# One list of steps up to the third batch's attention, one quad's sums moved to GpSimd, two late Q/K loads moved to ScalarE's queue

## The chip, the cores and the metric

The kernel runs on one core of a Trainium2 chip. The metric is the device time of one execution in microseconds (us); less is better. A core has five engines with an instruction queue each: TensorE (PE; its weight loads are listed as PEld), VectorE (DVE), ScalarE (ACT), GpSimd (POOL) and SyncE (SP). Each works through its own queue in program order and waits for the others by semaphores. DMA transfers are issued from the queues of SP, ACT and POOL.

## The reference

Cosine attention over 8 batches, 12 heads, 448 positions and 64 dimensions, followed by a two-layer network with an exact GELU. The heads of a batch lie side by side as 768 features of 3584 tokens.

```python
q_n = q / (np.linalg.norm(q, axis=-1, keepdims=True) + 1e-06)
k_n = k / (np.linalg.norm(k, axis=-1, keepdims=True) + 1e-06)
scores = np.matmul(q_n, k_n.transpose(0, 1, 3, 2)) / tau          # tau = 0.1
attn = np.exp(scores - np.max(scores, axis=-1, keepdims=True))
attn = attn / (np.sum(attn, axis=-1, keepdims=True) + 1e-09)
attn_out = np.matmul(attn, v)
x = attn_out.transpose(0, 2, 1, 3).reshape(B * S, H * D)          # 3584 x 768
h = x @ w_in                                                      # 768 -> 2048
g = 0.5 * h * (1.0 + erf(h / sqrt(2)))
out = g @ w_out                                                   # 2048 -> 768
```

## The kernel before

The heads are worked on in quads: 4 heads are one quad g, a batch is three quads, so there are 24 (g0 to g23). Batches are counted from 0 here: g0 to g2 are batch 0, g3 to g5 batch 1, g6 to g8 batch 2. A quad's 448 positions are seven chunks of 64.

**A quad's way.** `load_qk` brings Q and K (two DMAs of 448 KB) into one of four buffers; `square` (on ACT or POOL) and `reduce` (DVE) give the squared norms; `logs`, `roots` (ACT, logarithm and exponential, one table) and `inverses` (DVE) give one over the norm; `scale` (POOL) writes the normalised Q and K in bf16. They are turned either by PE (`transposes`, then `copies` by DVE out of PSUM) or, for most quads, by one DMA transpose from SP's queue. Then, chunk by chunk, `scores` (4 PE matmuls in 64x64 tiles into a pair of PSUM banks) and `exps` (ACT, one instruction for 128x896). `visit(p)` does scores and exponentials of the next chunk in pair p of three. The row sums are made on PE by `sums` (matmuls with ones, 16 a quad from batch 1 on) and turned on DVE (`turned`, `inverted`), or on POOL by `folded` (six additions of 128x896) followed by the longer `turned_all` and `inverted_all` on DVE. `values` weights V (28 PE matmuls), `spread` and `normalise` (DVE) write the batch's x. The squares and loads are numbered by unit: unit 0 and 1 are the halves of g0, unit n is g(n-1) from there on. The argument of `load_qk` is a quad.

**The network.** For each batch, 96 matmuls of 128x128x448 (16 row blocks m, six pieces kd of the 768 features) give h in PSUM banks, ACT applies the GELU into g. The output matmuls (128x384, 16 to a bank) of one batch are cut into single matmuls that are handed out between the `scores` of the next batch, as filling work; DVE copies a finished bank and SP stores it. ACT changes its table between exponentials and GELU; each change is one table load.

**Weights.** `load_wi(i)` brings w_in: 0 and 1 are features kd 0, 1 and kd 2, 3; 2 and 3 are kd 4, 5 for the first and second half of the columns. `load_wo(i)` brings w_out: 0 and 1 the two halves of kf for the first 384 output columns, 2 and 3 the same for the others. Both, and `load_v`, are issued from POOL's queue, which converts to bf16.

**The order of work.** The tile framework is told to keep the written order: each engine gets its instructions in the order in which the Python code calls the helpers. Batch 0's attention is a list of calls written out by hand (`attention_first`). What follows is code: `first(b)` for a batch's GELU layer, `attention(b, fill)` with branches for b = 1, b = 2 and the rest, and `upto(f, n)`, which calls a step for all units up to n that have not had it. In batch 1 every quad's sums are made on PE:

```python
    def both(g, p):
        total(g)
        weighted(g, p)
```

At the start `spin` gives PE matmuls without use, and `late` is a one-element POOL copy that reads g0's last K.

Of the kernel before, what the change touches and what calls it, by code (L numbers as in the profile page):

```python
# [9 lines left out]
F32 = mybir.dt.float32  # L10
# [6 lines left out]
def kernel(  # L17
# [108 lines left out]
    def load_qk(g):  # L126
        b, n = divmod(g, NQ)
        t = qkp.tile([128, 2, 2, C, D], F32, tag="qk", name=f"qk{g}")
        qk_t[g] = t
        for s0, s1 in ((0, 1), (1, 2)) if g == 0 else ((0, 2),):  # L130
            for i, src in enumerate((q, k)):
                eng = nc.scalar if g == 0 and s0 == 0 and i == 1 else nc.sync
                eng.dma_start(
                    out=t[:, i, s0:s1].rearrange("p s c d -> p s (c d)"),
                    in_=src[b, 4 * n + 2 * s0:4 * n + 2 * s1].rearrange(
                        "(s h) (p c) d -> (h p) s (c d)", h=2, c=C))
# [127 lines left out]

    def gathered(g, p):
# [58 lines left out]
    def values(g, chunks=range(C), p=None):  # L324
        for c in chunks:
            if c == 0 and g < NQ:
# [70 lines left out]
    def second_pieces(sb, t, ni):  # L397
        state = {}

        def mm(kf):  # L400
# [8 lines left out]
            if kf == KF - 1:  # L409
                nc.vector.tensor_copy(ot[:, ni * NH:(ni + 1) * NH], ps[:, :NH])  # L410
# [7 lines left out]
        return [lambda kf=kf: mm(kf) for kf in range(KF)]  # L418
# [46 lines left out]
    early = {}  # L465

# [5 lines left out]
    def attention_first():  # L472
        x_t[0] = xp.tile([128, KD, S], BF16, tag="x", name="x0")
        DV, AC, GP = nc.vector, nc.scalar, nc.gpsimd
        Q, K = 0, 1
        square(0, ((AC, Q),))
        square(0, ((AC, K),))
        reduce(0, Q)
        reduce(0, K)
        square(1, ((AC, Q),))  # L480
        upto(load_v, 1)
        logs(0)
        reduce(1, Q)
        roots(0)
        upto(load_wi, 1)
        square(1, ((AC, K),))
        inverses(0)
        square(2, ((AC, Q),))
        reduce(1, K)
        scale(0, ((GP, 1),))  # L490
        logs(1)
        reduce(2, Q)
        roots(1)
        scale(0, ((GP, 0),))
        spin(2)
        transposes(0, 1)
        square(2, ((AC, K),))
        inverses(1)
        spin(1)
        transposes(0, 0)  # L500
        square(3, ((AC, Q),))
        copies(0, 1)
        scale(1, ((GP, 0),))
        copies(0, 0)
        square(3, ((AC, K),))
        scale(1, ((GP, 1),))
        upto(load_qk, 5)
        spin(1)
        transposes(1, 0)
        reduce(2, K)  # L510
        scores(0, ((0, 0), (0, 1)))
        upto(load_v, 2)
        transposes(1, 1)
        copies(1, 0)
        logs(2)
        scores(0, ((0, 2), (0, 3)))
        roots(2)
        upto(load_wi, 2)
        exps(0, ((0, 0), (0, 1)))
        inverses(2)  # L520
        copies(1, 1)
        exps(0, ((0, 2), (0, 3)))
        spin(2)
        scores(0, ((0, 4), (0, 5)))
        scale(2, ((GP, 0),))
        reduce(3, Q)
        exps(0, ((0, 4), (0, 5)))
        spin(1)
        scores(0, ((1, 0), (1, 1)))
        reduce(3, K)  # L530
        exps(0, ((1, 0), (1, 1)))
        spin(1)
        scores(0, ((1, 2), (1, 3)))
        scale(2, ((GP, 1),))
        upto(load_qk, 6)
        transposes(2, 0)
        exps(0, ((1, 2), (1, 3)))
        sums(0, (0,))
        copies(2, 0)
        scores(0, ((1, 4), (1, 5)))  # L540
        logs(3)
        scores(0, ((0, 6), (1, 6)))
        roots(3)
        transposes(2, 1)
        exps(0, ((1, 4), (1, 5)))
        inverses(3)
        sums(0, (1,))
        scale(3, ((GP, 0),))
        copies(2, 1)
        sums(0, (2,))  # L550
        exps(0, ((0, 6), (1, 6)))
        sums(0, range(3, 5))
        scores(1, ((0, 0), (1, 0)))
        scores(1, ((0, 1), (1, 1)))
        sums(0, (5,))
        exps(1, ((0, 0), (1, 0)))
        sums(0, (6,))
        upto(load_wi, 3)
        transposes(3, 0)
        turned(0)  # L560
        exps(1, ((0, 1), (1, 1)))
        scores(1, ((0, 2), (1, 2)))
        values(0, (0,))
        scale(3, ((GP, 1),))
        upto(load_wi, 4)
        copies(3, 0)
        values(0, (1,))
        exps(1, ((0, 2), (1, 2)))
        values(0, (2,))
        scores(1, ((0, 3), (1, 3)))  # L570
        inverted(0)
        values(0, range(3, 5))
        spread(0, 1)
        values(0, (5,))
        exps(1, ((0, 3), (1, 3)))
        scores(1, ((0, 4), (1, 4)))
        values(0, (6,))
        spread(0, 0)
        sums(1, (0,))
        square(4, ((GP, K),))  # L580
        exps(1, ((0, 4), (1, 4)))
        sums(1, (1,))
        scores(1, ((0, 5), (1, 5)))
        normalise(0, 0)
        transposes(3, 1)
        exps(1, ((0, 5), (1, 5)))
        scores(1, ((0, 6), (1, 6)))
        copies(3, 1)
        sums(1, (2,))
        square(4, ((GP, Q),))  # L590
        square(5)
        upto(load_wo, 2)
        exps(1, ((0, 6), (1, 6)))
        sums(1, range(3, 5))
        normalise(0, 1)
        scores(2, ((0, 0), (1, 0)))
        sums(1, (5,))
        exps(2, ((0, 0), (1, 0)))
        sums(1, (6,))
        scores(2, ((0, 1), (1, 1)))  # L600
        turned(1)
        values(1, range(2))
        exps(2, ((0, 1), (1, 1)))
        values(1, (2,))
        scores(2, ((0, 2), (1, 2)))
        inverted(1)
        values(1, range(3, 5))
        spread(1, 0)
        values(1, (5,))
        exps(2, ((0, 2), (1, 2)))  # L610
        values(1, (6,))
        scores(2, ((0, 3), (1, 3)))
        sums(2, (0,))
        reduce(4, K)
        normalise(1, 0)
        exps(2, ((0, 3), (1, 3)))
        sums(2, (1,))
        scores(2, ((0, 4), (1, 4)))
        spread(1, 1)
        values(2, (0,))  # L620
        sums(2, (2,))
        exps(2, ((0, 4), (1, 4)))
        scores(2, ((0, 5), (1, 5)))
        normalise(1, 1)
        values(2, range(1, 3))
        exps(2, ((0, 5), (1, 5)))
        values(2, (3,))
        scores(2, ((0, 6), (1, 6)))
        exps(2, ((0, 6), (1, 6)))
        reduce(4, Q)  # L630
        spin(1)
        early[4] = mm_tile("hp0_4")[:, :S]
        w_in(0, early[4], 4, range(2))
        sums(2, range(3, 7))
        values(2, (4,))
        logs(4)
        turned(2)
        values(2, (5,))
        roots(4)
        values(2, (6,))  # L640
        inverted(2)
        inverses(4)
        scale(4)
        spread(2, 1)
        spread(2, 0)
        normalise(2, 1)
        normalise(2, 0)
        done.update({square: 6, reduce: 5, root: 5, scale: 5, transposes: 5})

# [49 lines left out]

    def attention(b, fill):
        fill = list(fill)
        if b == 1:
            parts = iter((20, 13, 14, 17, 16, 16))
        elif b == 2:
            parts = iter((22, 12, 12, 13, 11, 13, 11, 11, 11, 6, 6))
        elif len(fill) == 128:
            parts = iter((14, 22, 22, 26, 28, 16))
        else:  # L710
            parts = iter((14, 17, 13, 18, 18, 16))
# [28 lines left out]
        if b == 1:  # L740
            upto(scale, u + 3)
            upto(load_v, b + 2)
            upto(transposes, u + 3)
            upto(load_qk, g0 + NQ + 2)
            upto(square, u + 4)
            visit(0, 1, 2)
            run()
            visit(0, 1, 2)
            run()
            upto(load_qk, g0 + NQ + 3)  # L750
            visit(0, 1)
            upto(square, u + 5)
            run()
            visit(0, 1, 2)
            both(g0, 0)
            upto(load_v, b + 3)
            upto(load_qk, g0 + NQ + 4)
            visit(1, 2)
            upto(reduce, u + 4)
            run()  # L760
            visit(1, 2, 0)
            both(g0 + 1, 1)
            visit(2, 0)
            logs(6)
            roots(6)
            run()
            both(g0 + 2, 2)
            inverses(6)
            done[root] = 7
        elif b == 2:  # L770
            upto(scale, u + 3)
            upto(load_qk, g0 + 6)
            upto(transposes, u + 3)
            upto(scale, u + 4)
            upto(load_qk, g0 + 7)
            upto(transposes, u + 4)
            visit(0, 1, 2)
            run()
            visit(0, 1, 2)
            norms(9)  # L780
# [230 lines left out]
```

## Time and profile before

| | |
|---|---|
| runs | 402.37, 400.3, 406.49 us; median 402.37 |
| profiled execution | span 398.6 us from the first to the last instruction; 3.8 us less than the median of the runs, which also hold what lies around the span |
| busy | PE 392.0, PEld 207.8, DVE 264.0, ACT 267.8, POOL 250.6 us |
| granted TensorE clock | 0.999 on average |
| PE by kind | output matmuls 148.1 us, GELU layer 147.0, scores 46.0 and 9.5, values 24.2 and 17.5, sums 5.7 and 4.2, spins 8.7, transposes 5.5, last outputs 5.4 |
| DMA | 54.52 MB; hardware queue of SP 41.79 MB, software queue of POOL 11.80 MB |

A group's line gives engine, operation, out<-in by the program's names, shapes and count, then busy time and the mean of one in ns, then the idle time of the engine before it and what ended it. In a timeline the first column is the start, the second the length of the merged row. Rows of PE overlap by the depth of its pipeline, so what a row costs is the distance to the start of the next.

### The profile page before, as it was taken

Reading aid. Unit: us, or ns where it says so; the run is one execution under the profiler, and the core shown is the slowest. Engines: PE = TensorE matmul, PEld = TensorE weight load, DVE = VectorE, ACT = ScalarE, POOL = GpSimd, SP = SyncE. Lnnn points to the kernel's source line nnn. Section 1 sums busy time; section 2 is a strip of 40 time slices with the busy share of each in tenths; the row PEclk is TensorE's granted clock in tenths of the full one; section 3 lists DMA queues with packets and bytes.
Section 4 is the critical chain, followed back from the end, with each engine's and each line's share of the span. In section 5 each row is a group of like instructions: output and inputs, shape, how many; then the busy total and the mean of one; then the engine's idle time right before and its main releaser. Section 6 shows DMA issues by size and latency. Waiting matters only on the chain.

```text
span 398.6 us, 8027 instructions
## 1 busy us (share of the span) xinstructions
PE 392.0 (98%) x3245; PEld 207.8 (52%) x3245; DVE 264.0 (66%) x530; ACT 267.8 (67%) x399; POOL 250.6 (63%) x162
## 2 busy tenths in 40 slices
PE   7999999999999999999999999999999999999996
PEld 3444555555545555555555555555555555555564
DVE  5787214955487999589963999769973797461021
ACT  6995787557988877888665977889656756504300
POOL 5898814269699694959587394969768391920000
PEclk9999999999999999999999999999999999999999
DMA  8999999747296890678145591566024720130033
GB/s 290 261 258 217 205 233 308 154 106 226 50 254 234 158 230 2 178 150 207 70 105 138 126 240 38 162 113 147 2 27 101 148 46 2 41 77 3 1 80 80
DMA packets 66485, 54.52 MB, mean 137 GB/s; under 512 B 38672, under 2 KB 62352, under 8 KB 66448
## 3 DMA queue, kind: packets, MB, share of 16 engines
q1 hardware_dynamic: 54464, 41.79, 39.0%
q0 software_dynamic: 11600, 11.80, 18.8%
q8 instruction: 25, 0.41, 0.4%
q10 hardware_dynamic: 384, 0.43, 0.3%
q14 instruction: 12, 0.10, 0.1%
HBM read 45.61 MB, written 11.01 MB: 142 GB/s over the span
## 4 chain that ended last, share of the span: by engine, by line
PE 95%; issue 1%; DVE 1%; POOL 1%; ACT 0%; POOLq 0%
PE hp L469 37%; PE op L406 36%; PE st L242 9%; PE o L320 4%; PE o L335 4%; PE op L425 1%; PE sm L305 1%; PE sh L667 1%; PE tp L221 1%; PE sm L314 1%; PE spin L463 0%; POOL wi L441 0%; DVE nq L168 0%; POOL qkb L204 0%; POOL v L145 0%
## 5 line engine op out<-in xcount | busy, mean ns | idle before, releaser
L252 ACT ACTIVATE pt<-st 128x896 bf16<-128x896 f32 x155 | 132.5, 916 | 29.0 <-PE st L242 28.4
L406 PE MATMUL op<-wo,g 128*128 128x384 bf16 x864 | 148.1, 326 | 0.0
L469 PE MATMUL hp<-x,wi 128*128 128x448 bf16 x768 | 147.0, 353 | 0.1
L204 POOL TENSOR_TENSOR qkb<-qk,rn 128x896 bf16<-128x896 f32 (+1 forms) x50 | 80.2, 1628 | 66.3 <-DVE rn L188 64.9
L406 PEld LDWEIGHTS <-g 128*128 128x128 bf16 x864 | 81.4, 98 | 62.6 <-issue 11.2
L469 PEld LDWEIGHTS <-wi 128*128 128x128 bf16 x768 | 74.4, 98 | 71.1 <-issue 2.8
L263 POOL TENSOR_TENSOR acc<-acc,pt 128x896 f32<-128x896 f32 x55 | 103.8, 1887 | 4.3
L929 ACT ACTIVATE g<-hp 128x448 bf16<-128x448 f32 x128 | 63.6, 552 | 63.6 <-PE hp L469 63.5
L410 DVE COPY ot<-op 128x384 f32<-128x384 f32 x54 | 29.9, 555 | 83.1 <-PE op L406 80.8
L168 DVE TENSOR_REDUCE nq<-sq 128x14 f32<-128x896 f32 (+1 forms) x50 | 50.6, 1038 | 10.2 <-POOL sq L160 6.7
L242 PE MATMUL st<-qkT 64*64 64x448 bf16 x620 | 46.0, 356 | 0.2 <-ACT pt L252 0.2
L160 POOL TENSOR_TENSOR sq<-qk 128x896 f32<-128x896 f32 x18 | 29.9, 1683 | 16.3 <-DMA qk<-in_q_dram 10.9
L369 DVE TENSOR_TENSOR x<-o,rs 128x448 bf16<-128x448 f32 x48 | 28.0, 609 | 9.9 <-PE sh L667 6.4
L270 DVE TENSOR_TENSOR acc<-acc,pt 128x896 f32<-128x896 f32 x30 | 33.0, 1099 | 1.0
L158 ACT ACTIVATE sq<-qk 128x896 f32<-128x896 f32 (+1 forms) x32 | 27.8, 902 | 2.2 <-DMA qk<-in_q_dram 1.8
L364 DVE STREAM_TRANSPOSE rs<-rc 128x448 f32<-128x448 f32 x48 | 28.7, 626 | 0.6
L242 PEld LDWEIGHTS <-qkT 64*64 64x64 bf16 x620 | 17.9, 105 | 20.5 <-issue 12.7
L263 POOL TENSOR_TENSOR acc<-pt 128x896 f32<-128x896 bf16 x11 | 20.7, 1879 | 8.9 <-DVE x L369 8.9
L320 PE MATMUL o<-pt,v 64*64 64x448 bf16 x364 | 24.2, 351 | 0.0
L673 ACT ACTIVATE pt<-sh 128x448 bf16<-128x448 f32 x26 | 14.1, 544 | 9.2 <-PE sh L667 8.5
L276 DVE STREAM_TRANSPOSE ta<-acc 128x448 f32<-128x448 f32 x32 | 18.5, 617 | 0.2
L335 PE MATMUL o<-pt,v 64*64 64x448 bf16 x308 | 17.5, 351 | 0.5 <-DVE x L369 0.5
(54 smaller groups left out, 212.4 us busy)
## 6 DMA issues: line engine op xcount, KB each, us to landing
qk<-in_q_dram SPq DMA_DIRECT2D x23, 448.0 KB, 4.6
qk<-in_k_dram SPq DMA_DIRECT2D x23, 448.0 KB, 5.4
out_dram<-ot SPq DMA_DIRECT2D x48, 192.0 KB, 3.2
v<-in_v_dram POOLq DMA_DIRECT2D x7, 672.0 KB, 7.7
wo<-in_moe_w_out_dram POOLq DMA_DIRECT2D x4, 768.0 KB, 11.6
wi<-in_moe_w_in_dram POOLq DMA_DIRECT2D x4, 512.0 KB, 14.4
out_dram<-ot SPq DMA_DIRECT2D x12, 96.0 KB, 2.1
wi<-in_moe_w_in_dram POOLq DMA_DIRECT2D x4, 256.0 KB, 14.6
```

What stands on the lines that cost most here:

```text
L160: eng.tensor_tensor(sq, t, t, ALU.mult)
L168: nc.vector.tensor_reduce(nq_t[n][:, j, i], sq_t[g, i][:, s0:s1], mybir.AxisListType.X, ALU.add)
L204: eng.tensor_tensor(qkb[:, i, :, s0:s1].rearrange("p c s d -> p s c d"), t[:, i, s0:s1], rn[:, i].to_broadcast([128, s1 - s0, C, D]), ALU. ...
L242: nc.tensor.matmul(st[cols, n, :S], lhsT=qkT[rows, 1, c, cols], rhs=qkT[rows, 0, :, cols], start=True, stop=True, tile_position=(64 * s, 6 ...
L252: nc.scalar.activation(pt, st[:, :, :S], AF.Exp, scale=inv_tau)
L263: nc.gpsimd.tensor_tensor(acc_t[g], all_t[g][:, 0] if c == 1 else acc_t[g], all_t[g][:, c], ALU.add)
L270: nc.vector.tensor_tensor(acc_t[g], acc_t[g], all_t[g][:, c], ALU.add)
L320: nc.tensor.matmul(bank_t[g, h][64 * s:64 * (s + 1), :S], lhsT=v_t[g][rows, s, c, :], rhs=pt_t[g, s, c][rows], start=(c == 0), stop=(c == ...
L335: nc.tensor.matmul(bank_t[g, h][cols, :S], lhsT=v_t[g][rows, s, c, :], rhs=pt_t[g, s, c][rows], start=(c == 0), stop=(c == C - 1), tile_po ...
L406: nc.tensor.matmul(ps[:, :NH], lhsT=g_t[sb][:, kf, t * 128:(t + 1) * 128], rhs=wo[:, kf, ni * NH:(ni + 1) * NH], start=(kf == 0), stop=(kf ...
L469: nc.tensor.matmul(t, lhsT=wi[:, kd, m * 128:(m + 1) * 128], rhs=x_t[b][:, kd, :], start=(kd == 0), stop=(kd == KD - 1))
L929: nc.scalar.activation(g_t[sb][:, m, hf * S:(hf + 1) * S], hps.pop(m), AF.Gelu)
```

## The change

`attention_first`, the special cases of `first` for b = 0 and 1 and the branches of `attention` for b = 1 and 2 go. In their place `opening` is one list of 550 calls, from the first load to the end of batch 2's attention; `first(2)` and the later batches are as before. Helpers for single banks, matmul groups and GELUs (`bank`, `banks`, `mm`, `gelu`, `run`) let the list name them one at a time. Within the list: the first batches' squares, loads of weights and V, transposes and table loads stand in another order; the sums of g4 are made by `folded`; Q and K of g4 and g5 are loaded from ScalarE's queue after `roots(4)`; two output banks are evicted by ScalarE (`run(1, AC)`); g4's `values` come after all of batch 1's scores. Cut to its core:

```diff
-    def load_qk(g):
+    def load_qk(g, queue=None):
...
-                eng = nc.scalar if g == 0 and s0 == 0 and i == 1 else nc.sync
+                eng = queue or (nc.scalar if g == 0 and s0 == 0 and i == 1 else nc.sync)
...
-                nc.vector.tensor_copy(ot[:, ni * NH:(ni + 1) * NH], ps[:, :NH])
+                (nc.scalar.copy if eng is nc.scalar else nc.vector.tensor_copy)(ot[:, ni * NH:(ni + 1) * NH], ps[:, :NH])
...
+    def mm(b, m, k0, k1):
+        w_in(b, hps_t[b, m], m, range(k0, k1))
+    def gelu(b, m):
+        sb, hf = divmod(b, 2)
+        nc.scalar.activation(g_t[sb][:, m, hf * S:(hf + 1) * S], hps_t.pop((b, m)), AF.Gelu)
...
+    def opening():
+        spin(1)
+        load_qk(0)
+        square(1, ((GP, Q),))
+        table(EXP_SET)
...
+        load_qk(1)
+        load_v(0)
+        load_v(1)
+        square(0, ((AC, K),))
...
+        inverses(0)
+        load_wi(1)
+        reduce(1, K)
+        square(2, ((AC, Q),))
...
+        scale(0, ((GP, 1),))
+        inverses(1)
+        scale(0, ((GP, 0),))
...
+        scale(2, ((GP, 0),))
...
+        load_wi(0)
...
+        square(4, ((GP, Q),))
...
+        scale(3, ((GP, 0),))
...
+        scale(3, ((GP, 1),))
+        load_wi(3)
...
+        square(4, ((GP, K),))
...
+        exps(2, ((0, 6), (1, 6)))
+        bank(0, 4)
+        values(2, (3,))
...
+        logs(4)
+        roots(4)
+        load_qk(4, AC)
+        sums(2, (1,))
...
+        sums(2, (6,))
+        values(2, (4,))
...
+        values(2, (6,))
+        more(0)
+        normalise(2, 0)
+        load_wi(2)
+        bank(0, 5)
+        square(5, ((GP, Q),))
...
+        mm(0, 1, 0, 4)
+        mm(0, 4, 0, 2)
+        load_qk(5, AC)
...
+        mm(0, 0, 0, 4)
+        mm(0, 0, 4, 6)
...
+        late_copy()
+        square(5, ((AC, K),))
+        reduce(5, K)
+        load_wo(1)
+        gelu(0, 2)
+        mm(0, 5, 0, 6)
+        square(6, ((AC, Q),))
...
+        mm(0, 7, 0, 6)
+        gelu(0, 4)
+        scale(4, ((GP, K),))
+        transposes(4, 1)
...
+        square(6, ((GP, K),))
...
+        table(EXP_SET)
+        scale(4, ((GP, Q),))
+        load_wo(0)
+        mm(0, 9, 0, 6)
+        reduce(6, K)
+        logs(5)
+        roots(5)
+        table(GELU_SET)
+        gelu(0, 10)
+        transposes(4, 0)
...
+        copies(4, 0)
+        bank(0, 11)
+        reduce(7, K)
...
+        inverses(5)
...
+        load_v(2)
+        visit(2)
+        run(1)
+        scale(5, ((GP, Q),))
+        scale(5, ((GP, K),))
+        run(3)
+        load_wo(3)
+        run(5)
+        transposes(5)
...
+        sums(3)
+        load_wo(2)
+        turned(3)
...
+        folded(4, (1,))
+        folded(4, (2,))
...
+        folded(4, (6,))
+        turned_all(4)
+        inverted_all(4)
...
+        run(1, AC)
+        run(1)
+        visit(2)
+        visit(0)
+        values(4, p=1)
+        scale(7, ((GP, Q),))
+        table(GELU_SET)
+        values(5, p=2)
+        sums(5)
...
+    opening()
+    assert not todo_t, len(todo_t)
+    first(2)
+    for b in range(3, B):
+        attention(b, output_pieces(b - 1))
+        first(b)
```

## The prediction

> **What bounds the kernel now.** I read the page first (span, busy shares, chain that ended last), then the busy time by stretches, then the timelines of TensorE, ScalarE and GpSimd over the first 80 us, then the DMA landings.
>
> ```profile
> span 398.6 us, 8027 instructions
> ...
> PE 392.0 (98%) x3245; PEld 207.8 (52%) x3245; DVE 264.0 (66%) x530; ACT 267.8 (67%) x399; POOL 250.6 (63%) x162
> ...
> PE 95%; issue 1%; DVE 1%; POOL 1%; ACT 0%; POOLq 0%
> ```
>
> TensorE (PE) is busy for 392.0 of 398.6 us and carries 95% of the chain. By stretches:
>
> ```profile
> 2.00:4.00 2.00, 2.00 (x6) 0.82 (x6) 0.04 (x1) 0.48 (x1) 0.00 (x0) 1.00 0.92 296
> ...
> 10.00:20.00 10.00, 9.72 (x97) 4.45 (x98) 7.69 (x13) 9.14 (x15) 8.88 (x10) 1.00 1.10 261
> 20.00:30.00 10.00, 9.54 (x148) 4.46 (x147) 8.49 (x16) 9.37 (x12) 10.00 (x8) 1.00 1.10 258
> 30.00:40.00 10.00, 9.94 (x69) 4.69 (x64) 7.16 (x12) 5.95 (x12) 8.25 (x7) 1.00 1.20 216
> 40.00:50.00 10.00, 10.00 (x64) 5.55 (x63) 2.86 (x5) 7.08 (x12) 9.00 (x8) 1.00 1.31 205
> 50.00:60.00 10.00, 10.00 (x82) 5.04 (x81) 1.12 (x2) 8.66 (x11) 1.57 (x2) 1.00 1.22 233
> ```
>
> The first busy column is PE, the last three numbers are granted clock, DMA share and GB/s. Two different stages show. From 40 us on PE has no gap at all, so its time there is the sum of its instructions. Before 32 us its busy time says little: matmuls are issued in small groups with waits between them, while ScalarE is at 9.1 to 9.4 and GpSimd (POOL) at 8.9 to 10 of 10. The DMA engines are full (a share above 1) up to 60 us. The PE and ScalarE timelines tell what the early stage hangs on:
>
> ```profile
> 30.55 0.54 PE L469 MATMUL hp<-x,wi 128*128 128x448 bf16 x2
> 31.02 0.95 PE L305 MATMUL sm<-pt,ones 128*64 128x448 bf16 x8
> 31.89 0.76 PE L335 MATMUL o<-pt,v 64*64 64x448 bf16 x12
> 32.59 8.88 PE L469 MATMUL hp<-x,wi 128*128 128x448 bf16 x46
> ...
> 65.47 0.85 PE L314 MATMUL sm<-pt,ones 128*32 128x448 bf16 x16
> 66.25 1.52 PE L335 MATMUL o<-pt,v 64*64 64x448 bf16 x28
> ```
>
> ```profile
> 12.29 4.13 ACT L252 ACTIVATE pt<-st 128x896 bf16<-128x896 f32 x5
> ...
> 18.66 10.29 ACT L252 ACTIVATE pt<-st 128x896 bf16<-128x896 f32 x12 [0.16 <-PE st L242]
> 29.49 1.73 ACT L252 ACTIVATE pt<-st 128x896 bf16<-128x896 f32 x2 [0.55 <-PE st L242]
> ```
>
> ScalarE runs the first batch's 21 exponentials from 12.29 to 31.22, 0.857 us each in the long row (10.29 / 12). Right behind them PE sums and weights quad 2 and at 32.59 enters the first dense matmul block (46 in 8.88 us, 0.193 each). So the end is: start of that block, plus all PE work behind it, plus any hole that opens in it.
>
> **The change, part by part.**
>
> (1) PE work. The matmul sums of g4 (batch 1's second quad) go: 16 matmuls, from 65.47 to the next row at 66.25, **-0.8 us**. GpSimd takes six additions (g4 chunks 1 to 6) at 1887 ns, 11.3 us, in a stretch where it is busy 1.6 of 10. VectorE pays 4.0 us for turned_all and inverted_all (two transposes 0.61, one reduction 1.09, four of 0.17, four of 0.18, a reciprocal 0.33) for 2.0 before (0.65, 0.82, 0.21, 0.33): hidden, as it idles 80.8 us for output banks. Scores come in 10 groups in batch 1 for 8 now; a group of 12 takes 0.70 us to the next row, three times four matmuls at 0.19 are 0.57, so two more groups cost +0.2. The count of spins (29) and of all other matmuls is the same.
>
> (2) The opening. One half-quad square moves from ScalarE to GpSimd, and GpSimd issues load_v twice (0.89, 0.83) and load_wi (1.2 for its two) ahead of the first scale, for one load_v and one load_wi before. With the square from about 4.9 (0.9 by the half-size scale, 3.64 / 4) the first scale starts at 4.9 + 0.9 + 0.9 + 0.8 + 1.2 = 8.7 for 7.62 now, and the fourth ends at 12.3. The first scores need two of them: 10.5, plus a transpose 0.5, a copy 0.6, scores 0.5: exponentials from 12.15 for 12.29, because before they waited for a logarithm behind two squares. Then 21 x 0.857 = 18.0, logarithm and root 0.55, one wait for GpSimd's scale of quad 1 of 0.3: last exponential at 31.0. PE has then only one chunk of sums and three of values ahead (0.3 + 0.6; now three more chunks of sums): dense block at 31.9 for 32.59, **-0.7 us**. Bounds: if the exponentials slip by the whole 1.1 of the first scale, +0.4; -1.5 if their two waits (0.16 + 0.55) vanish also.
>
> (3) Weights and late Q, K. These are the edits that can open holes.
>
> ```profile
> L133 SPq DMA_DIRECT2D qk<-in_q_dram x25: 367/532/1453, 0.7 to 253.9; - x25
> ...
> DMA to landing us min/median/max: 3.3/5.0/17.0
> ...
> L448 POOL DMA_DIRECT2D wo<-in_moe_w_out_dram x4: 883/914/962, 30.0 to 41.1; - x4
> ...
> DMA to landing us min/median/max: 8.5/11.6/13.8
> ...
> L216 SPq DMA_TRANSPOSE qkT<-qkb x20: 1468/1496/8077, 46.3 to 318.9; - x20
> ...
> DMA to landing us min/median/max: 3.4/3.5/12.3
> ```
>
> These are the loads of Q and K, of w_out, and the DMA transposes, each with its time from issue to landing. The queues' own rows give rates: software queue alone 0.82 MB in 4 us (36 to 40 us), hardware queue alone 1.51 MB in 4 us; together they take turns (416 and 409 packets from 20 to 24).
>
> The last part of w_in that block 0 needs, load_wi(2), is now behind square(4) and scale(3) on GpSimd: 12.3 + 3.4 (two scales) + 1.2 (load_wi) + 1.7 (square) + 3.4 + 1.2 + 1.7 = 24.9 instead of 19.3. It is read when PE has done 20 matmuls of the block: 31.9 + 3.8 = 35.7. By the landing of the last two w_in loads (14.3 to 14.7) it comes at 39.5, a hole of 3.8; by the rates, 3.8 MB go through the software queue from 9 us on, 2.1 of them in 15 us shared with Q and K loads at 0.14 MB/us (0.45 and 0.67 MB in the 4 us from 20 and from 24), the rest at 0.2: 9 + 15 + 8.5 = 32.5, or 35 with 2 to 3 us lost between issues, none. I take none, since the 14 us were spent behind other weights and the loads of g4 and g5, which now leave at 31.5; only g6's leave SP early, at about 22, when scale(3) frees a buffer (counted in the 15 us).
>
> Those two leave from ScalarE's queue, after the last exponential and root: four issues of 0.41 (its one issue at 0.74 us), 1.6 us in an idle time of ScalarE (3.98 before the first gelu), so no cost there. But square(5) of Q on GpSimd waits for g4, and **behind it on GpSimd's queue stand** load_wo(1), scale(4,K), square(6,K), scale(4,Q), load_wo(0). With the median 5.0 the data lands at 36.5; 1.7 + 0.2 + 0.9 + 1.7 give scale(4,K) at 41.0. PE wants it for its transposes after 48 matmuls, at 31.9 + 9.2 = 41.1. At the 8.8 that g6's Q took at 50 us, beside load_v, it is 3.7 too late; only the tail of load_wi(2) is beside it here, so I take a landing of 6.0: **+0.9**. Then square 1.7 and scale 1.7 put load_wo(0) at 44.4. The first output matmul, run(1), stands behind 96 matmuls, two transposes (0.5 each) and three scores (0.7): 31.9 + 18.4 + 1.0 + 0.7 = 52.0. By its rows load_wo(0) lands 8.5 to 13.8 later, 52.9 to 58.2: a hole of 0.9 to 6.2. Those rows had 0.7 to 1.4 MB queued ahead (3.3 to 7 us at 0.2 MB/us); without that 5 to 7 are left, landing 49.5 to 51.5, none. I take **+0.5**.
>
> transposes(5), which makes g4's keys, moves from 46.3 to about 53 (its scale waits for inverses(5), on VectorE behind the copy of the last transposes and reduce(7,K), which ends at 48.9), and g4's first scores come after 30 output matmuls and 7 scores, at 58.1. The two DMA transposes of this stage landed in 8.3 and 12.3 us, later ones in 3.5: 56.5 to 65.3, a hole of 0 to 7.2. The 12.3 stood behind Q and K loads on the SP queue, which now are not ahead of it, and the first issued for 3.6 us; I take 5.5, **+0.4**. Holes overlap: PE that waited 2 us for one transfer finds the next landed. So they count as a maximum more than a sum, somewhat above the largest: **+1.5** for all, bounds 0 and 7.2.
>
> (4) The rest. Evicting two output banks on ScalarE (0.55 each) and the other squares there sit beside 26 us of PE work for some 20 of ScalarE. From batch 1's dense block on the list keeps the old order of matmuls, and the quads' normalised x is wanted after 11 output matmuls (1.9 us) plus five more among dense ones: VectorE's 3.3 behind sums(5) is covered.
>
> **Sum** against the profiled span: 398.6 - 0.8 + 0.2 - 0.7 + 1.5 = 398.8. The median of the runs, 402.4, is 3.8 above that span; kept, this gives 402.6 us.
>
> **Rivals.**
>
> *A visible hole, below 2%.* A landing comes at the middle of its rows (w_out 11.6, transpose 8.3, Q 8.8), 3 to 4 us late: 402.4 - 1.3 + 3 to 4, or 5 to 6 with a second one behind it: 404.5 to 407. For it: full DMA until 60 us. Against: less is queued ahead now.
>
> *The late Q and K hold up GpSimd.* One mechanism: g4 lands late from ScalarE's queue, square(5) blocks GpSimd, scale(4,K) and load_wo(0) slip, and PE stops before its transposes at 41 us. At the longest landing in the row, 17.0, data comes at 48.5, 12.0 late: 402.4 - 1.3 + 12.0 = 413.1 us. It passes 2% from a landing of 14.4 us. For it: that 17.0 occurred in this very stage, beside weights. Against: load_wi(2) should be the only competitor. In the trace PE's first spins ran 6 in 2 us, where 10.4 fit later, so a cold PE is nearly half as fast. The Trainium skill, "TensorE: Matmul & The Clock Gate", section "What's actually happening", says that one idle window of about 3.4 us puts the clock back to half until a busy window has passed; by that rule a hole of 12 us would cost up to 1.7 us more, 414.8. No run here shows it in mid-kernel.
>
> *The opening shrinks by far more.* Reaching 394 needs the dense block at 24 us. 21 exponentials of 0.857 cannot be done by then from 12 us on; only something unseen would do it: 393.
>
> *The additions do not save PE time* (the sums were in the shadow of something): 403.4, inside the forecast's case.
>
> **How the numbers follow.** Forecast (397 to 404.5) 0.52; hole below 2% 0.18; GpSimd held up 0.24; far shorter opening 0.06. The 2% (8 us) is about what a measurement of this kernel can tell from no change. So faster 0.06, same 0.70, slower 0.24. The range 396.5 to 411.5 leaves out the shorter opening and half of the third case.
>
> **What would show it.** Right: first dense matmul near 31.9, 64 of the 128x32 matmul sums in place of the 80 of L314, six more GpSimd additions, PE without idle rows over 1 us. Wrong: PE waiting for w_in at 36, for GpSimd's qkb at 41, for w_out at 52 or for qkT at 58 us; GpSimd's squares waiting on Q/K past 40 us; PE clock below 1 in mid-kernel.

## The result and the profile after

| | before | after |
|---|---|---|
| median of 6 runs each | 403.09 us | 414.62 us |
| profiled execution, span | 398.6 us | 411.7 us |
| ratio after / before | | 1.0334, interval 1.0302 to 1.0366 |

The changed kernel is slower by 3.3%. The ratio leaves out the runs of either kernel that lay more than 1.5% above its fastest (421.71 us after, for one), so it is not the ratio of the two medians. The page of the changed kernel's profile begins so (busy time and share by engine, then the granted clock in 40 slices, then the shares of the chain that ended last):

```profile
span 411.7 us, 8011 instructions
PE 394.4 (96%) x3229; PEld 207.9 (51%) x3229; DVE 265.3 (64%) x533; ACT 273.6 (66%) x407; POOL 251.1 (61%) x162
PEclk9999996999999999999999999999999999999999
PE 86%; DMA 5%; POOL 3%; ACT 3%; DVE 2%; issue 1%; DVEq 0%; POOLq 0%
```

PE's busy time rose by only 2.4 us while the span rose by 13.1, so most of the loss is idle PE. The chain that ended last, which held no DMA before, now holds 5% of it. And one slice of the clock, the seventh (62 to 72 us), is at six tenths. All three point at one place. PE's timeline there (start, length of the merged row, and in brackets the idle time before it with what ended it):

```profile
51.76 0.76 PE L242 MATMUL st<-qkT 64*64 64x448 bf16 x12
...
57.44 1.47 PE L411 MATMUL op<-wo,g 128*128 128x384 bf16 x8
64.66 0.96 PE L242 MATMUL st<-qkT 64*64 64x448 bf16 x8 [5.75 <-DMA qkT<-qkb]
65.55 1.50 PE L319 MATMUL sm<-pt,ones 128*32 128x448 bf16 x16
...
73.63 0.57 PE L242 MATMUL st<-qkT 64*64 64x448 bf16 x8
77.33 2.29 PE L411 MATMUL op<-wo,g 128*128 128x384 bf16 x13 [3.13 <-DMA wo<-in_moe_w_out_dram]
```

In the kernel before, PE worked through this place without a stop:

```profile
56.12 2.29 PE L406 MATMUL op<-wo,g 128*128 128x384 bf16 x13
58.33 0.76 PE L242 MATMUL st<-qkT 64*64 64x448 bf16 x12
59.03 2.45 PE L406 MATMUL op<-wo,g 128*128 128x384 bf16 x14
61.41 0.57 PE L242 MATMUL st<-qkT 64*64 64x448 bf16 x8
```

After, PE stops twice in batch 1's attention: 5.75 us for the turned keys of g4, then 3.13 us for the other half of w_out. Behind the first it runs at half speed: eight scores take 0.96 us at 64.66 and 0.57 at 73.63. The windows show it in their seventh figure, the granted clock (length, busy time and count of PE, PEld, DVE, ACT, POOL, then clock, DMA share, GB/s):

```profile
55.00:60.00 5.00, 3.91 (x32) 1.60 (x30) 1.55 (x2) 4.50 (x6) 3.09 (x3) 1.00 1.29 154
60.00:65.00 5.00, 0.34 (x4) 0.19 (x8) 0.00 (x0) 0.00 (x0) 0.00 (x0) 0.70 1.38 133
65.00:70.00 5.00, 5.00 (x43) 1.82 (x36) 2.72 (x9) 3.66 (x5) 2.80 (x2) 0.62 1.70 143
...
62.00:68.00 6.00, 3.34 (x33) 0.97 (x34) 0.85 (x3) 2.31 (x4) 0.88 (x1) 0.50 1.43 111
```

From 60 us until PE starts again at 64.66 no engine computes, while DMA is full. The last row, of a finer window, has the clock at 0.50. What the transfers do there is told by the landing rows (name, count, duration of the issuing instruction, then the time from issue to landing):

```profile
L453 POOL DMA_DIRECT2D wo<-in_moe_w_out_dram x4: 937/940/962, 37.5 to 57.2; - x4
DMA to landing us min/median/max: 7.6/10.5/20.1
...
L216 SPq DMA_TRANSPOSE qkT<-qkb x20: 1469/1498/6811, 53.0 to 331.2; - x20
DMA to landing us min/median/max: 3.4/4.4/16.3
```

The longest w_out load went from 13.8 to 20.1 us and the longest DMA transpose from 12.3 to 16.3, though the medians moved by about 1 us only (11.6 to 10.5, 3.5 to 4.4). Both extremes lie in this stage: the transpose of g4's keys, issued at 53.0 us, took 11.6, that of g5's, at 57.2, took 16.3; `load_wo(3)`, at 52.9, took 11.3 and `load_wo(2)`, at 57.2, took 20.1. The two transposes alone (duration of the issuing instruction in ns, then landing):

```profile
L216 SPq DMA_TRANSPOSE qkT<-qkb x2: 1606/3434/5261, 53.0 to 57.2; - x2
...
DMA to landing us min/median/max: 11.6/14.0/16.3
```

Each transpose leaves SP at the end of a pair of scales on GpSimd, and the next instruction on GpSimd's queue after that pair is a w_out load, so each pair starts together. The two queues then take turns, as the DMA view of 56 to 61 us shows (queue: packets, MB, share):

```profile
q0 software_dynamic: 818, 0.63, 87.2%
q1 hardware_dynamic: 829, 0.21, 43.9%
```

Nearly equal counts of packets, but the transposes' are some 256 bytes (0.21 MB / 829), and a transpose has some 1,800 of them (448 KB of bf16 for a quad's Q and K). The counts are not level everywhere: from 62 to 64 us they are 120 and 364, and why both queues moved less there stays open. In the kernel before, all four w_out loads had left GpSimd by 41.1 us and g4's transpose left SP at 46.3. In the view of the kernel before from 50 to 54 us the hardware queue, with that transpose, has most of the packets:

```profile
q1 hardware_dynamic: 1810, 0.46, 87.3%
q0 software_dynamic: 357, 0.26, 42.6%
```

**Where the 13.1 us went**, from the starts of PE's rows after, less those before: dense block of batch 0 -0.28; the way to batch 1's first scores +0.79; from there through batch 1's attention and dense block to batch 2's first scores +10.35; from batch 2's first scores to its dense block +1.42 (1.05 of it a wait for VectorE's write of x, up to 133.46 us); the end of the program +0.8. The 10.35 is 5.75 + 3.13 for the two waits, 2.07 for half speed (the work from 64.66 to 68.8 us in twice its time), less some 0.6, the remainder, which is about what the sums that left PE save.

These terms lie one behind the other on PE, but they are not independent causes. The 5% of DMA on the chain that ended last is one transfer, `load_wo(2)` (start and length):

```profile
57.15 20.13 DMA wo<-in_moe_w_out_dram
```

The chain runs through it and not through the wait for g4's keys. Without that wait and the half speed PE would have come to the other half of w_out at about 66.4 us (77.33 - 5.75 - 3.13 - 2.07), and a `load_wo(2)` that landed at the same 77.28 would by itself have held it for 10.9. This is an estimate from these rows; it supposes that the landing would not move.

### The profile page after: what moved, and what is told of

It reads as the page before. It is cut to its first block, busy times and chain, and to the rows that moved or that the text cites. A ratio compares the mean times of both kernels' runs of the same rounds, so it can differ in the third digit from the quotient of the medians.

```text
span 411.7 us, 8011 instructions
## 1 busy us (share of the span) xinstructions
PE 394.4 (96%) x3229; PEld 207.9 (51%) x3229; DVE 265.3 (64%) x533; ACT 273.6 (66%) x407; POOL 251.1 (61%) x162
## 4 chain that ended last, share of the span: by engine, by line
PE 86%; DMA 5%; POOL 3%; ACT 3%; DVE 2%; issue 1%; DVEq 0%; POOLq 0%
PE hp L472 33%; PE op L411 32%; PE st L242 7%; DMA wo<-in_moe_w_out_dram 5%; PE o L325 4%; PE o L340 3%; PE spin L468 2%; POOL qkb L204 2%; PE op L430 1%; PE sh L518 1%; ACT L480 1%; PE tp L221 1%; ACT pt L252 1%; ACT g L501 1%; PE sm L319 1%
## 5 line engine op out<-in xcount | busy, mean ns | idle before, releaser
L263 POOL TENSOR_TENSOR acc<-acc,pt 128x896 f32<-128x896 f32 x60 | 113.1, 1885 | 4.7
L415 DVE COPY ot<-op 128x384 f32<-128x384 f32 x52 | 28.9, 555 | 78.2 <-PE op L411 73.0
L242 PE MATMUL st<-qkT 64*64 64x448 bf16 x620 | 47.7, 362 | 7.2 <-DMA qkT<-qkb 5.8
L158 ACT ACTIVATE sq<-qk 128x896 f32<-128x896 f32 (+1 forms) x38 | 34.2, 921 | 4.3 <-DMA qk<-in_k_dram 1.8
L263 POOL TENSOR_TENSOR acc<-pt 128x896 f32<-128x896 bf16 x12 | 22.5, 1877 | 17.9 <-ACT pt L252 9.0
L160 POOL TENSOR_TENSOR sq<-qk 128x896 f32<-128x896 f32 (+1 forms) x12 | 19.3, 1623 | 19.7 <-DMA qk<-in_q_dram 15.5
L325 PE MATMUL o<-pt,v 64*64 64x448 bf16 x364 | 24.2, 351 | 0.0
L281 DVE STREAM_TRANSPOSE ta<-acc 128x448 f32<-128x448 f32 x34 | 19.6, 616 | 0.7 <-POOL acc L263 0.4
## 6 DMA issues: line engine op xcount, KB each, us to landing
wo<-in_moe_w_out_dram POOLq DMA_DIRECT2D x4, 768.0 KB, 10.5
```

The source lines that it names most:

```text
L158: eng.activation(sq, t, AF.Square)
L242: nc.tensor.matmul(st[cols, n, :S], lhsT=qkT[rows, 1, c, cols], rhs=qkT[rows, 0, :, cols], start=True, stop=True, tile_position=(64 * s, 6 ...
L263: nc.gpsimd.tensor_tensor(acc_t[g], all_t[g][:, 0] if c == 1 else acc_t[g], all_t[g][:, c], ALU.add)
L325: nc.tensor.matmul(bank_t[g, h][64 * s:64 * (s + 1), :S], lhsT=v_t[g][rows, s, c, :], rhs=pt_t[g, s, c][rows], start=(c == 0), stop=(c == ...
```

## The experiments

Two theories stood at the start. **A**: the transposes of g4 and g5 and the late w_out loads meet and delay one another. **B**: the late Q and K from ScalarE's queue delay GpSimd's scales, and all else follows. Diffs are against the changed kernel where nothing else is said. Medians of the kernel before, beside these runs, were 400.9 to 401.1 us.

**Q and K from SP, early (`e1_qk_from_sp`).** Part of the change undone.

```diff
         load_qk(3)
+        load_qk(4)
...
         scale(2, ((GP, 0),))
+        load_qk(5)
...
-        load_qk(4, AC)
...
-        load_qk(5, AC)
```

> The changed list, but Q and K of g4 and g5 leave from SP's queue early again (g4 behind g3, g5 behind the last scale of g1's successor). Theory A, the collision of the g4 and g5 DMA transposes with load_wo(3) and load_wo(2): GpSimd's squares no longer wait near 27 us, so load_wo(1) and load_wo(0) leave earlier, but scale(5) still waits for inverses(5) at about 49, so transposes and the two late load_wo still leave together near 53 and PE still stands 4 to 6 us at the first scores of g4 and about 3 us at the first output matmul of the second half: 412 to 415 us. Theory B, the late Q and K hold up all that follows on GpSimd: with them early the holes close, about 402 us.

Measured 414.74 us, ratio 1.0347 (1.0323 to 1.0371). Its PE timeline keeps both waits:

```profile
64.90 0.96 PE L242 MATMUL st<-qkT 64*64 64x448 bf16 x8 [5.73 <-DMA qkT<-qkb]
...
78.12 3.27 PE L411 MATMUL op<-wo,g 128*128 128x384 bf16 x13 [3.85 <-DMA wo<-in_moe_w_out_dram]
```

B falls for the change as it stands: with Q and K early, both waits stay.

**w_out early (`e2_wo_early`).** The other half.

```diff
         load_wi(2)
+        load_wo(0)
+        load_wo(1)
+        load_wo(2)
+        load_wo(3)
```

(and the four later calls removed)

> The changed list, but all four load_wo stand right behind load_wi(2), at about 27 us, where GpSimd idles 8.8 us; Q and K of g4 and g5 stay on ScalarE's queue at 32 us. Theory A: no w_out traffic is left at 53 us, the transposes land within 4 to 5 us, both holes go (5.75 and 3.1 us) and the half clock with them (2 us); but the late Q and K now share the DMA engines with w_out from 32 us, so that the transposes on PE at 41 us may wait 1 to 4 us: 402 to 406 us. Theory B: Q and K even later, so the hole at 58 us is as long or longer: 413 us or more.

Measured 410.32 us, 1.0238 (1.0217 to 1.0258). Both waits are gone, and the transposes, issued at 60.5 and 63.8 us, land in 3.5 and 3.4. These two leave 3.3 us apart, nearer than the 4.2 in the kernel after, so it is not each other's company that makes them slow there. But one new wait stands earlier on PE:

```profile
46.93 0.90 PE L221 MATMUL tp<-ident,qkb 128*128 128x128 bf16 x7 [4.66 <-ACT g L501]
```

PE waits there for banks that GELUs on ScalarE have to free. The chain of waits goes back from it: the GELUs stood behind ScalarE's square of g5's Q, and that Q, issued from ScalarE's queue at 33.62 us, took 11.42 to land, now that w_out shared the DMA engines with it. The clock is at 0.57 on average from 44 to 52 us. So A is right about the two waits, and early w_out alone trades them for a delay by late Q and K as in B, only that it stops ScalarE's queue where B had GpSimd's.

**Both early (`e3_both_early`).** The diffs of the first two together.

> Both edits together: Q and K of g4 and g5 from SP early, and all four load_wo behind load_wi(2). Theory A and B alike: both holes, the half clock and any wait at 41 us are gone, what is left of the change is one quad's sums less on PE: 401 to 403 us. If neither is right the holes stay and it is 410 us or more. The price that could show is load_wi(2) landing later than 36 us behind Q and K.

Measured 403.76 us, 1.0072 (1.0051 to 1.0094); the profiled span is 402.5, the clock 1.0 throughout. Of the 13.1 us, 9.2 are gone. Some of what is left, on PE:

```profile
37.52 5.46 PE L472 MATMUL hp<-x,wi 128*128 128x448 bf16 x28 [1.66 <-DMA wi<-in_moe_w_in_dram]
...
61.16 0.57 PE L242 MATMUL st<-qkT 64*64 64x448 bf16 x8 [0.84 <-DMA qkT<-qkb]
```

The first is the wait for `load_wi(2)` that the prediction had looked for at 36 us; it comes when other loads stand beside it.

**Matmuls without use in the first hole (`e4_spins_in_hole`).** `spin(28)` between `run(8)` and the `visit(1)` of g4's first scores, so that PE does not fall idle.

> The changed list with 28 further matmuls without use (5.4 us) put where PE stands still, ahead of g4's first scores. If the half clock after the hole (6.8 us of it in the profile, about 4 of them with work) costs time of its own, the clock stays at 1.0 and the time falls by about 2 us: 412.5 us. If the half clock costs nothing, since PE waits for w_out afterwards anyway, the time stays within 0.5 us of 414.6.

The time is unsettled: the four runs spread from 409.9 to 418.4 us, by more than the question. The profile, of the run of 416.64 us, still says something. The clock stayed at 1.00 from 62 to 76 us, so the half speed in the kernel after does come from the idle time. But PE stopped again for the same load:

```profile
77.77 4.34 PE L411 MATMUL op<-wo,g 128*128 128x384 bf16 x13 [3.31 <-DMA wo<-in_moe_w_out_dram]
```

It went on at 77.77, where the kernel after did at 77.33: in this execution what was saved ahead of `load_wo(2)` ran into the wait for it, and the half speed then followed that wait (0.57 on average from 76 to 84 us).

**Transposes on PE (`e5_pe_transposes`).** g4 and g5 turned by PE and copied by VectorE; the loads stay where they are.

```diff
-        transposes(5)
         run(7)
+        transposes(5, 1)
+        copies(5, 1)
+        transposes(5, 0)
+        copies(5, 0)
```

(the same for g5)

> The changed list, but g4 and g5 are turned by PE (28 small matmuls in four groups, about 0.45 us each, and four VectorE copies) where the two DMA transposes were; load_wo(3) and load_wo(2) leave at 53 and 57 us as in the changed kernel. Theory A (transposes and w_out slow each other down): with the transposes gone, load_wo(2) lands 7 to 8 us after its issue instead of 20, both holes go, and PE pays 1.8 us: 411.7 - 5.75 - 2.1 - 3.1 + 1.8, a span of 402.5, time 404.5 us. Rival, load_wo(2) is late because it is issued late behind GpSimd's scales: it lands near 77 us all the same and the time stays above 411 us.

Measured 411.41 us, 1.0227 (1.0148 to 1.0307). The half of A that only this run can show holds: without DMA transposes beside them `load_wo(2)` lands in 10.0 us in place of 20.1 and `load_wo(3)` in 9.5 for 11.3, though both leave as late as in the kernel after. The landing row of w_out:

```profile
DMA to landing us min/median/max: 9.5/10.5/11.1
```

The time is far above what was expected, because the removed waits left others:

```profile
55.03 4.16 PE L411 MATMUL op<-wo,g 128*128 128x384 bf16 x16 [1.95 <-DMA wo<-in_moe_w_out_dram]
...
68.86 0.55 PE L221 MATMUL tp<-ident,qkb 128*128 128x128 bf16 x7 [2.02 <-DVE ot L415]
```

`load_wo(0)` met g6's Q and K, which left SP at 44 us here, and PE's own transposes waited for a bank that VectorE had to empty. Behind each wait, of some 2 us, the clock was at half for 3.4 us. The transposes' own work on PE (some 2 us) comes on top.

**Only `load_wo(2)` and `load_wo(3)` earlier (`e11_wo_ahead_of_scale5`).** They move directly behind `load_wo(0)`, so that they no longer leave with the transposes but stand ahead of them.

```diff
         load_wo(0)
+        load_wo(2)
+        load_wo(3)
```

(and the two later calls removed)

> The changed list with only load_wo(2) and load_wo(3) moved, from behind scale(5) and scale(6) to directly behind load_wo(0) (45 us). They then go through the software queue from 50 to 58 us, so the g4 transpose at 53 us still meets w_out: it lands 10 us or more after its issue and PE's wait at 58 us stays (4 to 6 us, and the half clock behind it), but load_wo(2) lands by 62 us, so the wait for it at 74 us (3.1 us) goes: 411.5 us. If the order of issue alone mattered and not the meeting, both waits would go: about 403 us.

Measured 411.44 us, 1.0251 (1.0205 to 1.0297), as expected. The wait for w_out is gone, that for g4's keys is longer, since its transpose still takes 13.0 us beside the same loads:

```profile
65.48 0.96 PE L242 MATMUL st<-qkT 64*64 64x448 bf16 x8 [7.16 <-DMA qkT<-qkb]
```

So the first wait is a matter of what is still in the software queue when the transpose leaves, not of the order of the two issues.

**The collision in the kernel before (`e8_before_late_wo`).** There the late w_out loads move behind g4's DMA transpose.

```diff
-            upto(load_wo, 4)
...
                 if b == 0:
+                    upto(load_wo, 4)
```

> The kernel before, with one edit: load_wo(2) and load_wo(3) are issued behind the scale of g4, together with its DMA transpose (46 us), instead of 6 us earlier. Theory A: the two slow each other down here too: the transpose of g4 lands more than 10 us after its issue instead of 8.3 and the second load_wo 14 us or more after its issue; the scores of g4 are due at 58.7 us and the w_out half at about 68 us, so hardly any time is lost: 401 to 404 us. Rival: the transposes are slow only because two of them leave together; then the landings stay at 8 and 8 to 10 us.

Measured 407.24 us, 1.0113 (1.0021 to 1.0205). Its profile is of the longest of its runs, 413.05 us, in which the clock was already at 0.51 from 13 to 27 us; all that follows comes some 8 us later, so only landings and waits are read from it. In it g4's transpose takes 10.1 us, the slowest w_out load takes 19.4 us and the slowest transpose 19.6, and PE waits 3.05 us for w_out at 74.45. So long landings come with the placement, in the other kernel too. Its price was expected at next to nothing and came to 0.2 to 2.1%; that the slack behind those loads is smaller than I took it is likely, but not shown. g5's transpose, the slowest, also stood behind g6's Q and K on SP's queue.

**Four mended versions**, to see whether a version can beat both kernels. `e6_mended`: w_out early as above, g4's Q and K from SP, g5's left on ScalarE's queue, `inverses(5)` directly behind `roots(5)`.

> All four load_wo behind load_wi(2), Q and K of g4 from SP early, those of g5 still from ScalarE's queue, inverses(5) directly behind roots(5). Against the run with both edits early: load_wi(2) no longer shares with g5, so its 1.66 us hole at 36 us shrinks to below 0.5; scale(5) starts some 4 us earlier, so the 0.84 us hole at 61 us goes: a span of 400.2, time about 402 us, that is 0 to 0.5% above the kernel before or level with it. If g5's Q lands after 39.5 us PE waits for a gelu at 41 us instead and it stays at 403.5 us or more.

Measured 406.48 us, 1.0120 (1.0058 to 1.0182), with this wait, again for a GELU:

```profile
49.49 0.55 PE L221 MATMUL tp<-ident,qkb 128*128 128x128 bf16 x7 [2.98 <-ACT g L501]
```

Here g5's K came late, beside w_out and g6's loads: its square on GpSimd waited 9.77 us for it, to 44.12, the logarithm on ScalarE waited for that square, and the GELUs stood behind the logarithm.

`e7_mended_pe_sums`: the same with g4's sums on PE, as in the kernel before.

> The same, but the sums of g4 are made on PE again (16 matmuls, turned and inverted) and GpSimd's six additions are gone. If the additions are worth what the rows say, 0.8 us more than the run beside it. If the 0.7 us wait for the normalised x before batch 1's dense block comes from the longer VectorE work behind the additions, that wait goes and the two are level.

Measured 407.12 us, 1.0132 (1.0053 to 1.0210). That is 0.6 us above `e6_mended`, in line with the 0.8 of the 16 sums, but the intervals also allow no difference: unresolved by time.

`e9_timed_loads`: g4 from SP, g5 from ScalarE, `load_qk(6)` behind the scale of g4's Q, all w_out behind the scale of its K.

> The changed list with g4's Q and K from SP early, g5's from ScalarE's queue at 32 us, the load of g6 moved behind scale(4,Q) (some 41 us), all four load_wo behind scale(4,K) (34 us), inverses(5) behind roots(5). Each transfer then has the DMA engines nearly alone when it is due: load_wi(2) until 35, g5 from 33 to 37, w_out from 37 to 53, g6 beside it. The wait for load_wi(2) (1.66 us with both early), for a gelu at 41 to 49 us (2.98 in the mended run) and for the g4 transpose (0.84) go. Left are 0.7 and 0.6 us of waits for the normalised x: a span of 400, time about 401.8, within 0.5% of the kernel before. If the g4 transpose lands later than 10 us beside w_out, PE waits up to 2 us at 58 us: 403.5.

Measured 405.95 us, 1.0105 (1.0065 to 1.0144). The wait for w_in is gone. The transpose of g4, issued at 49.2 us, landed 12.9 later, beside w_out first and V after it:

```profile
62.09 0.57 PE L242 MATMUL st<-qkT 64*64 64x448 bf16 x8 [2.87 <-DMA qkT<-qkb]
```

`e10_no_scalar_queue`: `e3_both_early` with `load_qk(6)` and `inverses(5)` as in the last one.

> Both g4 and g5 from SP early and all load_wo behind load_wi(2), as in the run with both early, and the load of g6 behind scale(4,Q), inverses(5) behind roots(5). The 1.66 us wait for load_wi(2) stays, as g5 still shares with it; the 0.84 us at the g4 transpose goes or stays below 1: time 402.5 to 403.8 us, some 1 to 2 us above the run beside it. If ScalarE's queue were a loss by itself it would be the faster of the two.

Measured 405.48 us, 1.0101 (1.0061 to 1.0140); waits of 0.98 us for w_in, 1.58 for g4's keys (landing 11.6 us after their issue at 49.4), and two below 0.8. By time it is level with `e9_timed_loads`, which keeps one load on ScalarE's queue, though the two differ in the place of w_out as well. `e6_mended`, `e9_timed_loads` and `e10_no_scalar_queue` came out some 2 to 5 us above what was expected of them. None of the four, and no version tried here, is faster than the kernel before.

## Why the prediction was wrong

**The step that failed** is the landing of `transposes(5)`, together with the landing of `load_wo(2)`, which had no term. For `transposes(5)` the prediction had the issue right (about 53; 52.99) and the time by which PE needs it (58.1; 58.9), had rows of 3.5 to 12.3 us, and took 5.5 "because" the 12.3 stood behind Q and K on SP's queue and the first transpose issued for 3.6 us. It landed after 11.6, and the term came to 5.75 in place of 0.4. The reason given was half of what the kernel before shows. The 12.3 did stand behind Q and K: from 56 to 60 us 141 packets were under 512 bytes, from 60 to 64 us 1,746. And the first transpose's packets moved only when its issue had ended at 49.9 us. But both also stood beside the software queue, w_out's last and then V, and this was left out, though the change puts w_out loads right beside them. After, the issue of g4's transpose lasted only 1.6 us and no Q or K stood ahead, and it still took 11.6. The bound of 7.2 held; the value chosen from inside it did not.

**The term that was missing.** `load_wo(2)` and `load_wo(3)`, moved from 40 and 41 us to 57.2 and 52.9, were not priced at all, and no reason was given; only `load_wo(0)` was. `load_wo(2)` made the second wait, 3.13 us, and by the estimate above it would alone have cost about as much as both waits and the half speed.

**Holes as a maximum.** "PE that waited 2 us for one transfer finds the next landed" did not come true: after 5.75 us for g4's keys PE waited again. The two transfers slowed each other, and both were late. But the rule that the largest hole decides fits the estimate of 10.9; the largest one was just not among those priced. 8.9 us of waits and 2.1 of half clock stood where 1.5 was taken for all.

**Terms that came to nothing.** PE's transposes at 41.40 us and its first output matmul at 52.46 did not wait, so the 0.9 for g4's Q and the 0.5 for `load_wo(0)` were not needed. g6's Q and K left SP at 37.59 us, not at about 22: SP waited for `late`, which stands behind the square of g4's Q on GpSimd.

**The rivals.** "The late Q and K hold up GpSimd" gave 413.1, or 414.8 with the clock, against a median of 414.62, but its place and cause were others, so that the number came near is luck: g4's Q reached GpSimd at 35.77 us and the transposes at 41 did not wait. With the same cause removed in `e1_qk_from_sp` the time stayed. Late Q and K do stop PE where w_out is early (`e2_wo_early`, 4.66 us), over ScalarE's queue. "Visible hole" named the right rows (transpose, w_out) but took 5 to 6 us for two of them, where the waits were 8.9, and had no half clock. Two of the signs of being wrong came as listed: PE waiting for qkT at 58 us, and a clock below 1 in mid-kernel.

**The opening.** The first scale started at 8.61 (forecast 8.7), but the exponentials at 13.07, not 12.15. The dense block at 32.31 instead of 31.9 gives 0.28 us of the 0.7. `load_wi(2)`, issued at 25.7, made no hole, as taken.

**The sums on GpSimd.** The six additions more (72 rows for 66 in all) are hidden as said. The 16 PE sums are gone; with the regrouping PE has some 0.6 less in batch 1, as forecast (-0.8 + 0.2), though this is the remainder of the sum above and not measured by itself. `e7_mended_pe_sums` doesn't contradict it.

**The clock.** The Trainium skill, "TensorE: Matmul & The Clock Gate", section "What's actually happening", gives one idle window of some 3.4 us for falling to half and one busy window for coming back. The trace agrees in kind: PE stopped at 58.9, fell to half at 62.0, worked again from 64.66 and was back at 68.8, which cost 2.07 us. Here the prediction's "up to 1.7" was close, though attached to another hole. The row that it read for a cold PE, 6 spins from 2 to 4 us, has a granted clock of 1.00, so it does not show the half clock; the 0.50 from 62 to 68 us does.

## What to carry to other kernels

When a load is moved, list what else is on the DMA engines at its new time, in both directions: a DMA transpose of many small packets and a weight load by the software queue that left together made both late here, and a landing time read off a row is valid only for the company it had there. Price every issue that the edit moves, also the ones that nobody mentions, and carry each to the point where PE needs it: the one left out may be the one that decides. A wait that ends on PE costs more than itself where the clock falls, but filling it need not gain anything if the next late transfer stands right behind.

## What the runs showed of the hardware

- A DMA transpose of one quad landed in 3.4 and 3.5 us with next to nothing in the software queue (`e2_wo_early`) and in 11.6 and 16.3 beside w_out loads. The issuing instruction can last longer as well, and SP's queue stands meanwhile: 1.5 and 1.6 us in `e2_wo_early`, 1.6 for g4's and 5.3 for g5's in the kernel after.
- The Trainium skill, "DMA: Bandwidth & Descriptors", section "Queues, rings and completion order", says that each DMA engine goes round the queues that have work, a packet of each in turn. The 818 and 829 packets from 56 to 61 us agree, the 120 and 364 from 62 to 64 do not show it. That a w_out load took 20.1 us beside the transposes and 10.0 without them is from the runs.
- Half clock followed idle times of PE of 1.95 and 2.02 us (`e5_pe_transposes`, 3.4 us of half clock each), 2.87 (`e9_timed_loads`), 5.75 (the kernel after, 6.8 us of half clock) and 7.16 (`e11_wo_ahead_of_scale5`, 10.2), but not one of 3.13 (the second wait in the kernel after), 2.98 (`e6_mended`) or 1.66 (`e3_both_early`). Length alone does not decide it; what does stays open.
